# A new instruction order from a planner with a table of tile changes: top-k attention and a mixture of experts on one core

## The chip, the cores and the metric

The kernel runs on one core of a Trainium2 chip. TensorE (PE; PEld is its weight load), VectorE (DVE), ScalarE (ACT), GpSimd (POOL) and SyncE (SP, which here issues all the transfers) run side by side and meet at semaphores. The metric is the device time of one execution in microseconds (us), the median of several runs; lower is better.

## What is computed

For each of 8 batches and 8 heads (sequence 576, head width 64): scores, the 32 largest of each row kept, softmax over those, times v. The 8 heads side by side are the input x (576 x 512) of four small attention experts, each with a causal mask, and each row of x takes the two experts with the largest gate.

```python
scores = scale * np.matmul(q, k.transpose(0, 1, 3, 2))
kth = np.partition(scores, -top_k, axis=-1)[..., -top_k:-top_k + 1]
scores = np.where(scores >= kth, scores, -1000000000.0)
attn = softmax(scores)                      # top_k = 32
x = (attn @ v) as batch x 576 x 512
for e in range(E):                          # 4 experts
    q, k, v = x @ wq[e], x @ wk[e], x @ wv[e]
    a = softmax(np.where(causal, -1000000000.0, scale * (q @ k.transpose(0, 2, 1))))
    ye = a @ v @ wo[e]
    out += (gate weight of e where e is among the two chosen) * ye
```

## The kernel before

The work is cut into tasks. A task is a handful of instructions on one engine, with a duration written in the code, the tasks that it depends on, the buffers that it takes, and a priority. A planner (`Plan.order`) walks through time once when the program is built: at each step it looks, engine by engine, at the tasks that could start within `SLACK` ns of the earliest one, takes the one with the smallest priority number, and sets its end by the written duration. The order that comes out is the order of the instructions on each engine's queue. On the chip each engine works its queue strictly in that order and waits at semaphores; the planner's times are not kept. Priorities are a due time (pair of heads, plus offsets named `D_...`) plus a number for each kind of task (`BIAS`).

Two heads are one pair; 4 pairs make one batch; 32 pairs in all. Each pair has nine blocks of 128 rows (`j` = 0 to 8). The tasks that the prediction names:

- `scores` (TensorE, four matmuls into a PSUM slot, twice that for j = 4), `copy` (ScalarE, slot to SBUF `s3`), three blocks to a group.
- `f1`, `f3`, `f4`, `f5`, `win`, `rep` (VectorE): the top 32 of each row of one group of three blocks; `mask` (ScalarE).
- `s1` to `s9`: the softmax's sum. `s8` transposes it on TensorE and `s9` (ScalarE, line 726) writes it into rows of the operands that `st` reads.
- `st`: the transposed scores once more, with mask products; `exp` (ScalarE) into `pt`; `av`: times v, with 64-column weights; `neg` and `xh`, `xl`: the result as a high and a low part, x.
- Per batch, from the four pairs' x: `vproj` (5 tasks), `proj` (16), `neg2`, `s_stage` (the experts' scores), `m_stage` (VectorE, row maximum), `e_stage` (ScalarE, exponential), `t_stage` (transposes), `avm`, `c4`, `prod` (times wo), then the store.

In `s_stage` of a block t below 4, two experts are computed at once: six products with 64-row weights (`prods`), and two 128-row matmuls that add the causal mask (`causal`). In the kernel before, the planner's note `first` decides which comes first: `causal` if the task before on TensorE ended with what the planner calls short, `prods` otherwise. PSUM holds three slots and one accumulator; `s3` exists twice.

The planner knew one surcharge on TensorE:

```python
if short and t.kind not in (SHORT, TURN):
    dur += self.SWITCH          # 107 ns
t.first = short
short = t.kind in (SHORT, MIXED) or t.kind == EITHER and not short
```

Of the kernel before, what the change touches and what calls it, by code (L numbers as in the profile page):

```python
# [98 lines left out]
LONG, SHORT, EITHER, MIXED, TURN = 1, 2, 3, 4, 5  # L99


class Plan:
# [8 lines left out]
    SLACK = 35.5049  # L111
# [3 lines left out]
    SWITCH = 107.0  # L115
# [28 lines left out]
    def order(self):  # L144
        engs = {t.eng: [0.0, []] for t in self.tasks}
        port = {"DVE": -1e9, "POOL": -1e9}
        short = False
# [39 lines left out]
        while len(out) < len(self.tasks):  # L187
# [6 lines left out]
            s, _, _, t = best  # L194
# [39 lines left out]
def dve(n):  # L234
    return (n + 66) / 0.96


def pool(n):
# [5 lines left out]
BIAS = {"<lambda>": 23.740355, "again": 11.475029, "av": 0.361842, "avm": 11.263865, "c1": 7.177941, "c2": -23.286692,  # L244
        "c3": -10.384414, "c4": 6.710642, "c5": -28.708972, "cast": 24.64198, "cast_swap": -0.010375, "check1":
        -18.850708, "check2": 53.583539, "check3": -34.443475, "compare": 26.790953, "constants": 21.071669,
        "copy": -2.358499, "count": 28.676911, "diag": 14.816047, "dup": -1.633581, "dup1": -3.600648, "dup2":
# [4 lines left out]
        "load_swap": 2.335659, "loadv": -1.414793, "low_again": -18.468765, "m_stage": -40.332939, "mark":  # L252
        -1.554494, "mask": -0.719054, "neg": 2.485033, "neg2": -9.889744, "o_stage": -12.76194, "oh":
        -25.677682, "ol": 20.823251, "ot": -30.766377, "prod": 22.021447, "proj": 0.40995, "rep": -9.52529,
        "s1": -31.464437, "s2": -12.850911, "s3": -9.816986, "s4": -13.763698, "s6": -2.693483, "s7": -4.517811,
        "s8": -3.65251, "s9": -21.892878, "s_stage": 0.129474, "scores": -0.234018, "st": -0.066757, "store":
        -15.216484, "sub": 14.129481, "t_stage": -14.84831, "tails": 8.355447, "vproj": 1.194931, "win":
        11.080557, "xh": 7.528878, "xl": 7.883384}
D_K2 = 33.110076
D_PREP = -6.722199  # L260
D_SC = 0.592125
D_TIE = 20.447724
D_MASK = 0.804776
D_STAT = -3.65447
D_TAIL = 0.303862
D_STEP = 0.099275
D_MOE = 4.227275
D_LAST = 10.459609
D_PEN = 3.906984
D_SPAN = 4.076115  # L270
# [5 lines left out]
def kernel(ctx, tc, qk, vL, wq, wk, wv, wo, out):  # L276
# [122 lines left out]
    pl = Plan()  # L399
# [139 lines left out]
    def topk(w, general):  # L539
# [4 lines left out]
        for g in range(3):  # L544
# [5 lines left out]
            for n, j in enumerate(js):  # L550
# [9 lines left out]
                a = add("PE", 531 if j != 4 else 1063, scores, need, bufs=[sl, s3] + used(w, j), prio=0, kind=LONG)  # L560
# [52 lines left out]
            marks.append(add("POOL", 200, mark, [t], bufs=[c], prio=-9))  # L613
            compare_last()
            t = add("DVE", 6 * dve(72) - 45, f5, [t], bufs=[fa, c], prio=P0)
            tl = add("POOL", 200, tails, [t], bufs=[c], prio=0)
# [683 lines left out]
```

## Time and profile before

| | before |
|---|---|
| median of 3 runs | 1190.8 us (1190.08 to 1192.21) |
| the profiled execution | 1190.3 us, of which 1188.5 us from the first to the last instruction |
| TensorE busy | 1114.5 us, 94% |
| VectorE busy | 1058.8 us, 89% |
| ScalarE busy | 985.9 us, 83% |
| mean granted TensorE clock | 0.977 of full |

Busy time is the sum of instruction times; TensorE's instructions overlap and their ends are modelled, so its waits are better read as the distance between starts of successive blocks than as idle time.

### The profile page before, as it was taken

To read this page: it belongs to the slowest core of one execution; us is meant where nothing else is said; L and a number is where in the kernel's file an instruction comes from. 1 tells how busy PE (TensorE), PEld (TensorE's weight loads), DVE (VectorE), ACT (ScalarE), POOL (GpSimd) and SP (SyncE) were. 2 spreads that over 40 slices of the span, in tenths; PEclk is the share of its full clock that TensorE was granted. 3 is DMA by queue.
4 is the path that set the end of the run, shared out by engine and by line. 5 is a ranking of instruction groups with operands and counts; after the bars stand their busy time and mean duration, and the time that the engine had idled before them with its cause. 6 is when DMAs were issued, how large, how long until landed. Compare 5 with 4: busy or idle time off the path is not lost. (4 is left out here: it accounts for less than half of the span.)

```text
span 1188.5 us, 27952 instructions
## 1 busy us (share of the span) xinstructions
PE 1114.5 (94%) x9330; PEld 911.7 (77%) x9330; DVE 1058.8 (89%) x4457; ACT 985.9 (83%) x2050; POOL 374.8 (32%) x803
## 2 busy tenths in 40 slices
PE   3688799999999999999999999999999999999997
PEld 2466587877878778887878778787788878787785
DVE  7999999999999999999999999999999999999121
ACT  5687779789898888989888888988888898888554
POOL 4322221424324232253223332252322542232112
PEclk8688899999999999999999999999999999999999
DMA  7133332223432332333422233323423334220101
GB/s 198 49 92 92 92 85 74 57 72 100 114 91 68 88 101 71 82 93 87 135 69 73 64 102 105 91 78 82 115 63 82 83 101 122 67 73 15 44 5 44
DMA packets 45576, 98.54 MB, mean 83 GB/s; under 512 B 7792, under 2 KB 7792, under 8 KB 45424
## 3 DMA queue, kind: packets, MB, share of 16 engines
q1 hardware_dynamic: 45424, 96.67, 30.4%
q8 instruction: 76, 1.25, 0.5%
q14 instruction: 76, 0.62, 0.2%
HBM read 32.06 MB, written 9.44 MB: 35 GB/s over the span
## 5 line engine op out<-in xcount | busy, mean ns | idle before, releaser
L817 ACT ACTIVATE pt<-slot 128x576 f32<-128x576 f32 x288 | 183.8, 649 | 69.8 <-PE slot L291 67.5
L291 PE MATMUL slot<-opa,opa 128*128 128x256 f32 (+3 forms) x984 | 197.1, 324 | 26.1 <-ACT s L558 11.0
L648 ACT ACTIVATE mask<-s,top 128x576 bf16<-128x576 f32 x288 | 212.2, 772 | 7.3 <-DVE top L602 6.7
L590 POOL COPY scrap<-cand 128x1 f32<-128x1 f32 x96 | 18.0, 187 | 601.6 <-DVE cand L586 575.1
L291 PE MATMUL acc<-pt,vt 128*64 128x256 f32 (+3 forms) x1152 | 198.4, 423 | 1.2 <-ACT pt L817 1.2
L558 ACT ACTIVATE s<-slot 128x576 f32<-128x576 f32 x288 | 176.4, 653 | 19.4 <-PE slot L291 18.1
L291 PE MATMUL slot<-opb,opb 128*128 128x320 f32 (+1 forms) x960 | 182.7, 311 | 4.3 <-DMA opb<-raw 1.9
L291 PEld LDWEIGHTS slot<-opa,opa 128*128 128x128 f32 (+1 forms) x984 | 145.7, 195 | 45.0 <-ACT s L558 13.9
L291 PEld LDWEIGHTS slot<-opb,opb 128*128 128x128 f32 x960 | 143.6, 193 | 11.5 <-ACT opb L726 2.4
L602 DVE MAX8 top<-cand 128x8 f32<-128x160 f32 x576 | 147.6, 311 | 0.0
L291 PEld LDWEIGHTS acc<-pt,vt 128*64 128x64 f32 (+1 forms) x1152 | 89.5, 144 | 53.5 <-issue 16.8
L577 DVE MAX8 cand<-fb 128x8 f32<-128x288 f32 x288 | 130.5, 453 | 0.0
L291 PEld LDWEIGHTS <-mask 128*128 128x128 bf16 (+1 forms) x1632 | 78.1, 101 | 59.7 <-issue 49.8
L291 PE MATMUL slot<-negi,mask 128*128 128x128 bf16 (+3 forms) x1632 | 121.3, 217 | 0.3 <-ACT pt L817 0.2
L569 DVE TENSOR_TENSOR fa<-s 128x864 f32<-128x864 f32 x96 | 107.3, 1118 | 10.5 <-ACT s L558 10.5
L572 DVE TENSOR_TENSOR fb<-s 128x864 f32<-128x864 f32 x96 | 101.4, 1056 | 0.0
L628 POOL TENSOR_TENSOR ind<-cand,top 128x486 bf16<-128x486 f32 x96 | 96.2, 1002 | 7.1 <-ACT ind L636 6.9
L602 DVE MAX8 top<-oct 128x8 f32<-128x72 f32 x576 | 93.8, 218 | 0.0
L607 DVE MATCH_REPLACE8 cand<-top,cand 128x160 f32<-128x160 f32 x288 | 86.1, 309 | 0.0
L636 ACT ACTIVATE ind<-ind,tiny 128x486 bf16<-128x486 bf16 (+1 forms) x96 | 67.5, 703 | 8.3 <-POOL ind L628 7.0
L291 PE MATMUL slot<-opa,k2a 128*128 128x256 f32 (+1 forms) x320 | 69.3, 298 | 2.8 <-ACT opa L726 2.8
L291 PE MATMUL slot<-opb,k2b 128*128 128x320 f32 x320 | 70.3, 301 | 0.5
(191 smaller groups left out, 2393.4 us busy)
## 6 DMA issues: line engine op xcount, KB each, us to landing
raw<-in_qk_dram SPq DMA_DIRECT2D x31, 576.0 KB, 3.7
opb<-raw SPq DMA_DIRECT2D x93, 144.0 KB, 3.3
opa<-raw SPq DMA_DIRECT2D x93, 144.0 KB, 2.4
vt<-in_vL_dram SPq DMA_DIRECT2D x32, 320.0 KB, 3.4
opb<-opb SPq DMA_DIRECT2D x62, 144.0 KB, 2.6
opa<-opa SPq DMA_DIRECT2D x62, 144.0 KB, 2.4
out_dram<-pr SPq DMA_DIRECT2D x32, 256.0 KB, 2.0
k2a<-opa SPq DMA_DIRECT2D x32, 144.0 KB, 2.3
```

The costliest lines, as they stand in the source:

```text
L291: nc.tensor.matmul(o, l, r, start=start, stop=stop, skip_group_check=True)
L558: nc.scalar.activation(s3.t[:, n], sl.t[:, o0:o0 + S], AF.Copy)
L569: v.tensor_tensor(out=fa.t, in0=s3.t[:, :, 0:288], in1=s3.t[:, :, 288:576], op=OP.max)
L572: v.tensor_tensor(out=fb.t, in0=s3.t[:, :, 0:288], in1=s3.t[:, :, 288:576], op=OP.min)
L577: v.max(out=c.t[:, n, 152:160], in_=fb.t[:, n])
L590: nc.gpsimd.tensor_copy(scrap[:, g:g + 1], c.t[:, 0, 143:144])
L602: v.max(out=w.top.t[0][:, j, 8 * r:8 * r + 8], in_=oc.t[:, n] if r < 2 else c.t[:, n, 0:160])
L607: v.match_replace(out=c.t[:, n, 0:72] if r == 1 else src, in_values=src, imm_value=LOW, in_to_replace=w.top.t[0][:, j, 8 * r:8 * r + 8])
L628: nc.gpsimd.tensor_tensor(out=ind.t[:, 0:486].rearrange("p (a n) -> p a n", a=3), in0=c.t, in1=m32[:, js[0]:js[0] + 3, 31:32].to_broadcast ...
L636: nc.scalar.activation(ind.t[:, 0:n], ind.t[:, 0:n], AF.Sign, bias=tiny, accum_out=signs[:, 3 * w.p + g:3 * w.p + g + 1])
L648: nc.scalar.activation(w.mask[j].t, s3.t[:, n], AF.Relu, bias=w.top.t[0][:, j, 31:32], scale=-1.0)
L817: es[j] = add("ACT", act(S), lambda sl=sl, pt=pt, o0=o0: nc.scalar.activation(pt.t, sl.t[:, o0:o0 + S], AF.Exp, scale=0.125), [a], bufs=[s ...
```

## The change

Four things are edited. The surcharge becomes a table by what stood before on TensorE (`COST`, with two new kinds: `AV` for tasks with 64-column weights, `ROW` for `s_stage` below block 4). Many written durations are new. `s_stage` has `causal` first always. `f3` and `f4` no longer wait, in the planner, for GpSimd. And all the priorities (`BIAS`, `D_...`, `SLACK`) are other numbers, so that the order of the instructions on every engine is another; the instructions themselves, their operands and shapes are the same.

```diff
-    SLACK = 35.5049
+    SLACK = 58.114
-    SWITCH = 107.0
+    COST = ((0, 0, 0, 0, 0, 0, 0, 0), (0, 0, 8, 0, 0, 0, 98, 0), (0, 78, 0, 144, 150, 0, 110, 82),
+            (0, 80, 26, 82, 80, 0, 10, 28), (0, 129, 100, 115, 130, 0, 0, 53), (0, 173, 70, 65, 100, 0, 107, 0))
+    NEXT = {LONG: 1, SHORT: 2, MIXED: 3, AV: 4, ROW: 5}
...
-                elif e == "DVE" and t.tag in self.PORT:
+                elif e == "DVE" and t.tag in self.PORT and t.tag not in ("f3", "f4"):
...
-                if short and t.kind not in (SHORT, TURN):
-                    dur += self.SWITCH
-                t.first = short
-                short = t.kind in (SHORT, MIXED) or t.kind == EITHER and not short
+                dur += self.COST[state][t.kind]
+                t.first = state > 1
+                state = self.NEXT.get(t.kind, 1 if t.first else 3)
...
-BIAS = {"<lambda>": 23.740355, "again": 11.475029, "av": 0.361842, "avm": 11.263865, "c1": 7.177941, "c2": -23.286692,
+BIAS = {"<lambda>": 383.78, "again": -295.6731, "av": 1.0033, "avm": 620.4783, "c1": 108.4144, "c2": -154.7034,
...
-            a = add("PE", 1020 if j != 4 else 790, lambda j=j, pts=pts: av(j, pts), [es[k] for k in jj] + [w.v, a],
-                    bufs=pts + [acc, w.vt], prio=1, tag="av", kind=SHORT)
+            a = add("PE", 1070 if j != 4 else 727, lambda j=j, pts=pts: av(j, pts), [es[k] for k in jj] + [w.v, a],
+                    bufs=pts + [acc, w.vt], prio=1, tag="av", kind=AV)
...
-            t = add("DVE", 6 * dve(72) - 45, f5, [t], bufs=[fa, c], prio=P0)
+            t = add("DVE", 3 * dve(144) - 22, f5, [t], bufs=[fa, c], prio=P0)
...
-                        order = (causal, prods) if pl.first else (prods, causal)
-                        order[0](True)
-                        order[1](False)
+                        causal(True)
+                        prods(False)
...
-                        kind=EITHER if t < 4 else MIXED)
+                        kind=ROW if t < 4 else MIXED)
...
-                pe = (190, 360, 600, 810, 520)[t]
+                pe = (217, 430, 658, 825, 468)[t]
```

Three places show how instructions move. The first is VectorE at the program's start, before and after as one difference. Line 469 and line 499 make the low parts of the first pair's operands, lines 380 to 395 (most of them stand unchanged in the part left out) the constants, line 569 is the first `f1`.

```order
+L469 TENSOR_TENSOR opa_0_69<-raw_68,opa_2_71 64x576
+L469 TENSOR_TENSOR opa_1_70<-raw_68,opa_2_71 64x576
 L469 TENSOR_TENSOR opb_0_78<-raw_68,opb_2_80 64x576
 L469 TENSOR_TENSOR opb_1_79<-raw_68,opb_2_80 64x576
-L469 TENSOR_TENSOR opa_0_69<-raw_68,opa_2_71 64x576
-L469 TENSOR_TENSOR opa_1_70<-raw_68,opa_2_71 64x576
-L499 TENSOR_TENSOR opa_2_71<-pr_144,opa_0_69 64x576
 L380 TENSOR_SCALAR identf<-ptm_0_149 128x128
 L380 TENSOR_SCALAR identb<-ptm_0_149 128x128
```

Line 499 of `opa` stood ahead of all the constants and now stands behind them, just ahead of line 499 of `opb`. At the same place ScalarE's queue (the casts of the next pair are line 462, the copies of the first three score blocks line 558 with `s_87`) changes as follows:

```order
 L415 ACTIVATE wv_199<-ot_154 128x1040
 L558 ACTIVATE s_87<-slot_64 128x576
+L462 ACTIVATE opa_2_74<-raw_68 128x576
 L558 ACTIVATE s_87<-slot_65 128x576
 L462 ACTIVATE opb_2_83<-raw_68 128x576
 L558 ACTIVATE s_87<-slot_66 128x576
 L558 ACTIVATE s_88<-slot_64 128x576
-L462 ACTIVATE opa_2_74<-raw_68 128x576
 L558 ACTIVATE s_88<-slot_65 128x576
```

A cast, which needs the next pair's load, has moved between the first and the second copy. On SyncE the load of v (line 514) has moved ahead of the first load of q and k (line 458).

The second place is TensorE in the middle of the program, behind an `s8` (line 722). Before, one `scores` (`opb_1`, `opb_0`) stands between it and the `st` (`opb_0`, `opb_1`) that reads what `s9` writes:

```order
L722 MATMUL slot_65<-identf,stat_2_119 4x128 x4
L291 MATMUL slot_66<-opb_1_79,opb_0_78 128x320
L291 MATMUL slot_66<-opb_1_79,opb_0_78 128x256
L291 MATMUL slot_66<-opb_1_79,opb_2_80 128x320
L291 MATMUL slot_66<-opb_1_79,opb_2_80 128x256
L291 MATMUL slot_65<-opb_0_81,opb_1_82 128x320
L291 MATMUL slot_65<-opb_0_81,opb_1_82 128x256
```

In the change, at the same point of the batch's rhythm, a `neg2` (`negr`) and a `proj` (`wk`) stand between them:

```order
L722 MATMUL slot_65<-identf,stat_2_119 4x128 x4
L291 MATMUL slot_66<-qk_0_133,negr 128x288 x2
L291 MATMUL slot_64<-x_0_125,wk_197 128x288 x2
L291 MATMUL slot_64<-x_1_126,wk_197 128x288 x2
L291 MATMUL slot_64<-x_0_125,wk_198 128x288 x2
L291 MATMUL slot_65<-opb_0_81,opb_1_82 128x320
L291 MATMUL slot_65<-opb_0_81,opb_1_82 128x256
```

So the `st` has two blocks ahead of it where it had one.

The third place is TensorE at the first `s_stage` of the second two experts. Before, its products (`qk`) are followed by two `scores` and an `av` (`acc`), and, further on, by an `st`, before its transposes:

```order
L291 MATMUL slot_64<-qk_2_135,qk_0_133 128x128 x2
L291 MATMUL slot_64<-qk_2_135,qk_1_134 128x128 x2
L291 MATMUL slot_64<-qk_3_136,qk_0_133 128x128 x2
L291 MATMUL slot_65<-opb_1_82,opb_0_81 128x320
L291 MATMUL slot_65<-opb_1_82,opb_0_81 128x256
L291 MATMUL slot_65<-opb_1_82,opb_2_83 128x320
L291 MATMUL slot_65<-opb_1_82,opb_2_83 128x256
L291 MATMUL slot_66<-opb_1_82,opb_0_81 128x320
```

In the change the next `s_stage` (causal pair first: `tri`, `identb`) and one `av` stand between them and the transposes (`pr`); these rows begin inside that next `s_stage`, behind its causal pair:

```order
L291 MATMUL slot_64<-qk_2_135,qk_0_133 128x256 x2
L291 MATMUL slot_64<-qk_2_135,qk_1_134 128x256 x2
L291 MATMUL slot_64<-qk_3_136,qk_0_133 128x256 x2
L291 MATMUL acc_67<-pt_121,vt_86 64x256
L291 MATMUL acc_67<-pt_122,vt_86 64x256
L291 MATMUL acc_67<-pt_122,vt_86 64x320
L291 MATMUL acc_67<-pt_121,vt_86 64x320
L1077 MATMUL slot_66<-identf,pr_144 128x128 x2
```

Four blocks between the first scores and their transposes have become two.

## Rows read from the trace of the kernel before

**Rows 1.** The page: busy time, share of the span and instructions of each engine.

```profile
PE 1114.5 (94%) x9330; PEld 911.7 (77%) x9330; DVE 1058.8 (89%) x4457; ACT 985.9 (83%) x2050; POOL 374.8 (32%) x803
```

**Rows 2.** Windows: stretch, length, busy us of each engine (instructions), granted clock, DMA.

```profile
8.50:162.40 153.90, 113.49 (x762) 86.94 (x763) 146.39 (x643) 113.30 (x213) 44.81 (x82) 0.83 0.34 90
162.40:290.90 128.50, 123.03 (x1060) 101.03 (x1059) 122.26 (x523) 111.20 (x237) 46.33 (x96) 1.00 0.32 84
580.20:718.10 137.90, 136.43 (x1168) 112.34 (x1167) 131.48 (x554) 121.91 (x256) 45.94 (x98) 1.00 0.33 88
1086.00:1188.50 102.50, 91.09 (x788) 74.59 (x786) 27.34 (x83) 57.88 (x130) 19.00 (x45) 0.98 0.10 31
```

**Rows 3.** Timeline of VectorE at the start: start us, us, instructions [idle before <-releaser].

```profile
8.54 0.23 DVE L380 TENSOR_SCALAR identf<-ptm 128x128 f32<-128x128 int32 x1
...
10.36 0.17 DVE L395 MEMSET sm<- 128x128 f32 x1
...
14.59 1.06 DVE L569 TENSOR_TENSOR fa<-s 128x864 f32<-128x864 f32 x1 [3.27 <-ACT s L558]
...
24.14 1.55 DVE L569 TENSOR_TENSOR fa<-s 128x864 f32<-128x864 f32 x1
```

**Rows 4.** Timeline of ScalarE at the start.

```profile
10.84 1.19 ACT L558 ACTIVATE s<-slot 128x576 f32<-128x576 f32 x2
13.33 0.68 ACT L462 ACTIVATE opb<-raw 128x576 fp32r<-128x576 f32 x1 [1.30 <-DMA raw<-in_qk_dram]
```

**Rows 5.** Timeline of SyncE's DMA issues at the start.

```profile
1.66 0.43 SPq L514 DMA_DIRECT2D vt<-in_vL_dram  x1
```

**Rows 6.** Timeline of TensorE in a middle batch: blocks that follow each other without a wait.

```profile
701.79 1.64 PE L291 MATMUL slot<-wo,qk 128*128 128x512 f32 x6
703.27 1.76 PE L291 MATMUL slot<-opb,opb 128*128 128x320 f32 x12
704.96 1.19 PE L291 MATMUL acc<-pt,vt 128*64 128x256 f32 x8
706.08 0.43 PE L291 MATMUL slot<-negi,mask 128*128 128x64 bf16 x5
...
716.69 2.92 PE L291 MATMUL slot<-wo,qk 128*128 128x512 f32 x12
719.45 0.38 PE L722 MATMUL slot<-identf,stat 128*4 128x128 f32 x2
```

**Rows 7.** Timeline of TensorE in the same batch: four places with a wait.

```profile
621.90 0.53 PE L291 MATMUL acc<-x,negr 128*128 128x256 f32 x2
623.02 1.33 PE L291 MATMUL slot<-opa,opa 128*128 128x256 f32 x8 [0.59 <-DVE v L903]
...
625.96 0.77 PE L291 MATMUL slot<-opb,opb 128*128 128x320 f32 x4
626.88 0.53 PE L291 MATMUL slot<-opb,opb 128*128 128x320 f32 x2 [0.15 <-ACT opb L726]
...
692.58 0.43 PE L291 MATMUL slot<-negi,mask 128*128 128x64 bf16 x5
693.25 0.53 PE L291 MATMUL slot<-opa,opa 128*128 128x256 f32 x2 [0.24 <-ACT pt L817]
...
698.76 1.48 PE L291 MATMUL acc<-pt,vt 128*64 128x256 f32 x8
700.17 0.43 PE L291 MATMUL slot<-negi,mask 128*128 128x64 bf16 x5
```

**Rows 8.** Timeline of all engines at two `s_stage` (`tri`) and an `av` (`acc`).

```profile
604.39 0.27 PE L291 MATMUL slot<-tri,identb 128*128 128x128 bf16 x2
...
605.19 0.42 DVE L1058 TENSOR_REDUCE sm<-slot 128x2 f32<-128x256 f32 x1 [0.43 <-PE slot L291]
...
605.70 1.19 PE L291 MATMUL acc<-pt,vt 128*64 128x256 f32 x8
...
606.83 0.20 ACT L1067 ACTIVATION_READ_ACCUMULATOR pr<-slot,sm 128x1 f32 x1
```

More of the change, by code (lines that the diff above doesn't have):

```diff
@@ L242 @@
 PEF = 1.0
-BIAS = {"<lambda>": 23.740355, "again": 11.475029, "av": 0.361842, "avm": 11.263865, "c1": 7.177941, "c2": -23.286692,
-        "c3": -10.384414, "c4": 6.710642, "c5": -28.708972, "cast": 24.64198, "cast_swap": -0.010375, "check1":
-        -18.850708, "check2": 53.583539, "check3": -34.443475, "compare": 26.790953, "constants": 21.071669,
-        "copy": -2.358499, "count": 28.676911, "diag": 14.816047, "dup": -1.633581, "dup1": -3.600648, "dup2":
[4 rows of a table removed]
[L252 to L270, printed above, removed]
+BIAS = {"<lambda>": 383.78, "again": -295.6731, "av": 1.0033, "avm": 620.4783, "c1": 108.4144, "c2": -154.7034,
+        "c3": 64.2277, "c4": -414.2653, "c5": 75.0207, "cast": 374.6002, "cast_swap": 813.697, "check1": -137.7188,
+        "check2": 169.9271, "check3": 340.7893, "compare": -163.741, "constants": -66.1999, "copy": 26.3246,
+        "count": 98.315, "diag": 265.3045, "dup": 94.8531, "dup1": -364.0748, "dup2": -451.9729, "e_stage": -66.8741,
[3 rows of a table added]
+        "g8": -623.0459, "g9": -194.0866, "load_": -134.7895, "load_swap": 123.308, "loadv": -319.0325,
+        "low_again": 144.4132, "m_stage": -426.4806, "mark": 504.7814, "mask": 51.3137, "neg": -637.0257,
[3 rows of a table added]
+        "st": -0.0455, "store": 502.323, "sub": -280.9441, "t_stage": -203.2947, "tails": -31.1234,
+        "vproj": -213.9761, "win": 38.661, "xh": 185.7676, "xl": 179.4791}
@@ L271 @@
+D_K2 = -9.24057
+D_PREP = -11.27653
+D_SC = 0.55092
+D_TIE = 371.38654
+D_MASK = 2.84383
+D_STAT = -42.02577
+D_TAIL = 0.31469
+D_STEP = 0.09921
+D_MOE = 4.98429
+D_LAST = 10.17993
+D_PEN = 4.21246
+D_SPAN = 4.11854
 MP = (14,3)
@@ L559, in topk @@
                 need = w.scores[0] + w.scores[1] if j == 4 else w.scores[0 if j < 4 else 1]
-                a = add("PE", 531 if j != 4 else 1063, scores, need, bufs=[sl, s3] + used(w, j), prio=0, kind=LONG)
+                a = add("PE", 525 if j != 4 else 1061, scores, need, bufs=[sl, s3] + used(w, j), prio=0, kind=LONG)
                 cps.append(add("ACT", act(S), copy, [a], bufs=[sl, s3], prio=0))
@@ L641, in later @@
                 pl.due += 0.3
-                counts.append(add("ACT", act(516, False, 1, 1), count, [a], bufs=[ind], prio=1))
+                counts.append(add("ACT", act(489, False, 1, 1), count, [a], bufs=[ind], prio=1))
                 pl.due = keep
@@ L831, in neg @@
                 mm(acc.t[:, 256 + c0:256 + c1], negr, xb.t[0][:, c0:c1], stop=True)
-        a = add("PE", 250, neg, [c], bufs=[acc, xb], prio=1, kind=LONG)
+        a = add("PE", 264, neg, [c], bufs=[acc, xb], prio=1, kind=LONG)
         d = add("ACT", act(S), lambda: nc.scalar.activation(xb.t[1][:, 0:S], av_(), AF.Copy), [a], bufs=[acc, xb], prio=1, tag="xl")
@@ L904, in moe @@
             when(1440)
-            a = add("PE", 1436, vproj, last + wd["v"], bufs=[sl, v2] + xbs, prio=3, kind=LONG)
+            a = add("PE", 1430, vproj, last + wd["v"], bufs=[sl, v2] + xbs, prio=3, kind=LONG)
             e1 = add("ACT", act(256), ev, [a], bufs=[sl, v2], prio=3)
@@ L997, in moe @@
                     when(800)
-                    a = add("PE", 795, proj, last + wd[name] + [a], bufs=[sl, qk] + xbs, prio=3, kind=LONG)
+                    a = add("PE", 787, proj, last + wd[name] + [a], bufs=[sl, qk] + xbs, prio=3, kind=LONG)
                 def ev1(sl=sl, k=k, qk=qk):
@@ L1009, in moe @@
                 c = add("ACT", act(S), ev1, [a], bufs=[sl, qk], prio=3)
-                a = add("PE", 260, neg, [c], bufs=[sl, qk], prio=3, tag="neg2", kind=LONG)
+                a = add("PE", 265, neg, [c], bufs=[sl, qk], prio=3, tag="neg2", kind=LONG)
                 d = add("ACT", act(S), ev2, [a], bufs=[sl, qk], prio=3)
@@ L1189, in moe @@
             when(1470)
-            a = add("PE", 1385, prod, split + wd["o"], bufs=[sl, oo, o], prio=3, kind=LONG)
+            a = add("PE", 1375, prod, split + wd["o"], bufs=[sl, oo, o], prio=3, kind=LONG)
             a = add("ACT", act(512), ev, [a], bufs=[sl, o], prio=3, tag="evo")
```

28 lines of the change are left out of this document (14 added, 14 removed), and 10 rows, old and new, of the table BIAS.

## The prediction

> **What bounds the kernel now.** I read the page first, then windows by stage, then TensorE's timeline inside one batch, then the start. The page shows two nearly full engines [rows 1]: TensorE at 94% and VectorE at 89%. An average over stages says little, so the windows come next [rows 2]. Four stages differ.
>
> - To 162 us there is no expert work yet. VectorE is busy 146.4 of 153.9 us and sets the pace; the granted clock averages 0.83, so TensorE spends about a third of this stage at the lower of its two levels, 1.2 GHz, and still waits. Making TensorE's order better buys nothing here; delaying VectorE costs its full delay.
> - From 162 to 291 us the first expert work comes in; TensorE 123.0 of 128.5 us (95.7%).
> - Then come the batches in the middle, all with the same rhythm; one of them takes 137.9 us, TensorE 136.4, VectorE 131.5, ScalarE 121.9, granted clock 1.00.
> - From 1086 us the last scores are out; VectorE has almost nothing left, TensorE works off the rest.
>
> In the middle, TensorE's busy time is too kind, since the modelled ends cover waits. I therefore price a block by the distance from its start to the next block's start where nothing waits [rows 6]: `prod` 2.76 us for two = 1.38; a `prod` behind the mask products of an `st` 1.48, so that such a change costs 0.10; three `scores` ahead of an `av` 1.69, which with the same 0.10 makes 0.53 for one; `av` 1.12. A `scores` streams 1152 columns, so other full-width blocks follow by their columns: `neg` or `neg2` with 576 takes 0.27, `proj` with 1728 takes 0.79. Against these prices the same batch shows waits [rows 7]: `neg` takes 1.12 us (0.85 too long, the next `scores` has no slot yet); a `scores` behind `s8` 0.92 us (0.53 and one change of 0.10; 0.29 too long, the `st` behind it waits for `s9`); the mask products of an `st`, 576 columns, 0.67 us (0.40 too long by the columns' price, of which the row prints 0.24 as idle: no free slot until an `exp` has read one); an `av` 1.41 us (0.29 too long). The pair `s8`, `scores`, `st` occurs twice a batch in the old order. Together 0.85 + 2 x 0.29 + 0.40 + 0.29 = 2.12 us a batch, and smaller ones beside them that I put at as much again at most. So TensorE bounds the middle, with 2 to 4 us of 137.9 lost to waits, and VectorE, 6.4 us short of full, is close behind.
>
> **The change part by part.**
>
> *The causal pair first, and the tile changes.* An `s_stage` crosses from 128-row to 64-row weights once inside itself whichever part is first; only its neighbours decide what it adds outside. 34 of 80 `s_stage` blocks turn round. I counted block pairs in both orders (they are the same 1281 blocks). Full-width work behind the 64-row products falls from 13 to 1 pairs (two changes' worth, 0.20 us: -2.4 us), full-width behind `av` from 45 to 33 (-1.2), behind transposes from 76 to 61 (-1.5), `av` behind full-width from 92 to 83 (-0.9), full-width behind mask products rises from 51 to 65 (+1.4). That is -4.6 us. Against it stand pairs that the trace prices poorly or not at all: a causal pair behind 64-row products (0 to 24 pairs), transposes behind them (1 to 16), transposes behind `av` (15 to 34). Bounds: nothing, or two changes (0.20) for the first and one (0.10) for the others: 0 to +8.2 us. Sum -4.6 to +3.6; I take the middle, **-0.5 us**.
>
> A second count looks at the weights' shapes alone (128 x 128, 128 x 64, 64 x 128, 128 x 4), transposes included in the first: a middle batch has 68 changes of shape in both orders, the whole program 540 before and 551 after; at the 0.10 us of [rows 6] for each that is +1.1 us, inside these bounds. The Trainium skill, TensorEngine Tiling (Array Packing), section Tiling Modes, says that a change of tiling mode, not of tile alone, drains the engine. The trace agrees as far as [rows 6] go, and by that rule the second count would be the right one: +1.1 us instead of -0.5.
>
> *The start.* Three moves on VectorE's path. The low part of `opa` (line 499), which the second half of the first `scores` reads, now stands behind the constants, which run from 8.54 to 10.53 us [rows 3]. The first `f1` begins at 14.59 after 3.27 us of waiting for the third copy. The ScalarE cast that waits until 13.33 us for the next pair's load [rows 4] now stands ahead of the second copy, so copies two and three come behind it and behind a second cast: 13.33 + 0.68 + 0.65 + 0.68 + 0.65 = 15.99 instead of 14.59, 1.4 us later. And the load of v is issued first, 0.43 us [rows 5], which may move the load chain too. I take **+1.7 us**; bounds 0 (the constants fill VectorE's 3.27 us of idle time and the load lands earlier) and +2.5. VectorE is full from there to 162 us, so nothing takes it back.
>
> *Experts earlier.* In the new order the first `vproj` stands 8 blocks behind the fourth pair's `neg`; in the old one 57. TensorE's idle time in 162 to 291 us, 5.5 us, can shrink to the middle's rate (1.5 of 137.9 gives 1.4): up to -4.1 us. I take half, **-2.0 us**; bounds -4.1 and 0.
>
> *Waits in the middle.* No edit removes a wait by itself; the order decides. What I can place: the two s9 waits go, because behind `s8` there now stand at least two blocks (for instance `neg2` and `proj`, 0.27 + 0.79 = 1.06 us, against the 0.92 after which the `st` could start [rows 7]): -0.58. For the slot and `exp` waits (0.85, 0.40, 0.29) the order has other neighbours and I cannot tell, so half: -0.77. What speaks for that half: the written durations come nearer to the trace. `av` is now written 1070 ns and 53 to 130 for what follows (1020 before, and 107 at most; the row has 1120), `neg` 264 (250; 270 by columns), and one group of VectorE's top 32, f1 to the last `win`, adds up to 9.57 us (was 9.82; 24.14 - 14.59 = 9.55 [rows 3]). The old order was laid out for a VectorE that would be slower and a TensorE that would be faster than they are; the new one keeps ScalarE and VectorE nearer to what TensorE needs. For the smaller waits I take -0.65. A new one arises: in the second two experts the first transposes have only an `s_stage` and an `av` between them and their scores. Two such `s_stage` blocks take 605.70 - 604.39 = 1.31 us, so these two 0.66 + 1.12 = 1.78; the chain from the maximum to the second sum took 605.19 to 607.03 = 1.84 us, and the products must end before it [rows 8]. At least 0.06 is missing, 0.3 with a handover of 0.24 as behind `exp` [rows 7]; I put in half of 0.3, +0.15. Sum -1.85 us a batch. The stretch from 162 to 1086 us is 924 / 137.9 = 6.7 batches: **-12.4 us**. Bounds: all named waits and as much again in small ones go, 4.2 x 6.7 = -28; or new waits equal the old ones, 0.
>
> *GpSimd and f3, f4.* That rule is the planner's alone and moves places only. `f1` takes 1.06 us in one row and 1.55 in another [rows 3]; a few such extensions more are covered by VectorE's 6.4 us of slack a batch, so 0; without that cover each would cost its 0.5.
>
> *The end.* TensorE-bound; the same blocks in another order, 0 (bounds -2 to +4, since ten more blocks stand behind the last `scores` than before, and only 11.4 us of the last 102.5 are idle).
>
> Sum: 1190.3 + 1.7 - 0.5 - 2.0 - 12.4 = 1177.1 us for the profiled execution. The median of the runs lies 0.5 above it, so **1177.6 us**.
>
> **The rivals.**
>
> *It only moves the waits* (chance 0.13). Counted by shapes nothing is gained in tile changes (+1.1), and three slots with ScalarE at 121.9 of 137.9 us [rows 2] make TensorE wait somewhere in any order. Then 1190.8 + 1.7 + 1.1 - 2.0 = 1191.6 us, within 0.2% of before, which is about what a measurement of this kernel can tell from no change. Against it: the s9 waits have a cause that the new order takes away.
>
> *VectorE starves* (chance 0.18). A batch has 160 TensorE blocks, 0.86 us each. The longest run of blocks without a `scores` grows from 13 to 19 of them, 11.2 to 16.4 us. Three `scores` and their last copy add 1.6 + 0.65, so 18.6 us pass between one group's arrival and the next one's; a group keeps VectorE for 9.55 us, the five row maxima in that run for about 3 (my estimate from 0.42 for the smallest [rows 8]). With two `s3` buffers a full stock covers it; a group that arrives just in time leaves up to 6 us of idle time. At half of that, and with today's 6.4 us of idle unchanged, a batch takes 3 us more: 1190.8 + 1.7 + 3 x 6.7 = 1212.6 us. It decides from the point on where VectorE idles more than 6.4 us a batch.
>
> *Nearly all waits go* (chance 0.12). TensorE then runs at its blocks' prices, bounded by VectorE's 131.5: 1190.8 + 1.7 - 0.5 - 2.0 - 28 = 1162.0 us.
>
> **How the numbers follow.** The forecast's own case, waits reduced by 0.7 to 3.3 us a batch, has 0.57: its time runs from 1168 to 1185 (1190.8 + 1.7 - 0.5 - 2.0 = 1190.0, less 22 or 5). With the last rival's 0.12 faster has 0.69; within 0.2% (1188.4 to 1193.2) has 0.13, slower 0.18. The range 1163 to 1193 leaves out the upper part of the starving case, about 0.15, and half of the last rival, about 0.05.
>
> **What would show it.** A middle batch of 136.0 us instead of 137.9; no line with TensorE idle before an `st` and released by line 726; the first `f1` near 16.3 us; the first `vproj` 49 blocks of 0.86 us, some 40 us, earlier than before; TensorE's changes of tile no cheaper in sum. The prediction is wrong if the batch stays at 137 or more, or if VectorE's busy share in a batch falls while TensorE's does too.

## The result, and the profile after

The median of the changed kernel is 1175.65 us (1174.58 to 1176.66, 4 runs), that of the kernel before 1190.68; the ratio is 0.9872, with a 95% interval from 0.9855 to 0.9889. The profiled execution took 1176.66 us, 13.6 us less than the one of before; 13.2 were forecast for it.

The first line is from the page: the busy time of each engine.

```profile
PE 1101.2 (94%) x9330; PEld 908.0 (77%) x9330; DVE 1057.8 (90%) x4457; ACT 983.5 (84%) x2050; POOL 371.7 (32%) x803
```

Against [rows 1] the work of VectorE and ScalarE is the same and the shares barely move; the span is shorter. To see where, I divide both traces at marks, the `neg` of each batch's last pair. Windows of the changed kernel between such marks (columns as in [rows 2]): the first two batches with expert work, one in the middle, and the end.

```profile
163.60:299.20 135.60, 130.98 (x1136) 107.81 (x1136) 129.31 (x551) 118.64 (x250) 47.33 (x97) 1.00 0.31 82
299.20:438.20 139.00, 137.73 (x1183) 113.85 (x1182) 134.38 (x571) 124.14 (x261) 46.59 (x100) 1.00 0.34 90
573.70:708.90 135.20, 134.50 (x1167) 111.83 (x1167) 130.78 (x554) 121.05 (x256) 44.88 (x98) 1.00 0.34 90
1109.80:1174.90 65.10, 55.61 (x469) 47.77 (x468) 11.71 (x25) 31.41 (x75) 10.81 (x29) 0.98 0.09 31
```

The marks stand at 162.4, 303.0, 440.7, ... 1123.2 us before and at 163.6, 299.2, 438.2, ... 1109.8 us after. So the start costs 1.2 us in these two traces, the seven batches in between give 960.8 - 946.2 = 14.6 us, and the end 65.3 - 65.1 = 0.2 us. The first mark alone is unsteady: of the kernels below, three with the queues of before up to it reach it at 159.3, 160.4 and 163.7 us, and three with the changed kernel's queues at 161.6, 162.2 and 163.0. The means of four traces each, 161.5 and 162.6, differ by about as much as the pair does, but a difference of 1 or 2 us at this mark between two single traces says little. The batches in the middle repeat better, within 0.4 us (137.7 to 137.9 before, 135.1 to 135.5 after, but for two that are named below). A batch in the middle went from 137.9 [rows 2] to 135.2 us. Its 2.7 us can be written down for each engine: VectorE's idle time fell from 6.4 to 4.4 us and its busy time by 0.7, TensorE's idle time by 0.8 and its busy time by 1.9, ScalarE's by 1.8 and 0.9.

On TensorE, as the distance from each block's start to the next block's start, such a batch consists of:

| us a batch | before | after |
|---|---|---|
| `neg` (4) | 2.35 | 1.06 |
| `scores` (36) | 24.55 | 23.32 |
| `st` (32, without block 4) | 27.43 | 26.69 |
| `s8`, `vproj`, `proj` (29) | 24.70 | 24.00 |
| `s_stage` of blocks below 4 (8) | 6.65 | 7.03 |
| `t_stage` (10) | 5.96 | 6.54 |
| `av` (20) | 21.56 | 21.86 |
| all others | 24.68 | 24.77 |
| sum | 137.88 | 135.27 |

Two of the places whose waits were named ahead of the result, in TensorE's timeline: first `neg` (`acc`, `negr`), then `s8` and the `st` that needs it:

```profile
603.14 0.43 PE L291 MATMUL acc<-x,negr 128*128 128x256 f32 x2
603.40 0.55 PE L291 MATMUL slot<-opa,opa 128*128 128x256 f32 x3
...
611.61 0.60 PE L722 MATMUL slot<-identf,stat 128*4 128x128 f32 x4
611.97 0.51 PE L291 MATMUL slot<-qk,negr 128*128 128x288 f32 x2
612.31 0.95 PE L291 MATMUL slot<-x,wk 128*128 128x288 f32 x6
613.11 0.42 PE L291 MATMUL slot<-opb,opb 128*128 128x320 f32 x2
```

`neg` takes 0.26 us to the next `scores` where it took 1.12 [rows 7]; all four of the batch take 0.26 to 0.27. Behind `s8`, `neg2` takes 0.34 and `proj` 0.80 us, and the `st` starts with no idle time. In the whole trace TensorE waits for line 726 twice, 0.7 us together; before, it was eight times, 3.5 us.

The start: VectorE's first `f1`, then ScalarE's casts (462) and copies (558), from the timelines of the two engines.

```profile
16.99 1.06 DVE L569 TENSOR_TENSOR fa<-s 128x864 f32<-128x864 f32 x1 [2.52 <-ACT s L558]
```

```profile
14.62 0.68 ACT L462 ACTIVATE opa<-raw 128x576 fp32r<-128x576 f32 x1 [1.44 <-DMA raw<-in_qk_dram]
15.21 0.63 ACT L558 ACTIVATE s<-slot 128x576 f32<-128x576 f32 x1
15.74 0.67 ACT L462 ACTIVATE opb<-raw 128x576 fp32r<-128x576 f32 x1
16.32 2.26 ACT L558 ACTIVATE s<-slot 128x576 f32<-128x576 f32 x4
```

As the order said, the second copy stands behind a cast that waits for the load, and the first `f1` begins at 16.99 instead of 14.59 us [rows 3].

### The profile page after: what moved, and what is told of

It is laid out like the page before. It is cut to its first block, busy times and chain, and to the rows that moved or that the text cites. A ratio compares the mean times of both kernels' runs of the same rounds, so it can differ in the third digit from the quotient of the medians.

```text
span 1174.9 us, 27936 instructions
## 1 busy us (share of the span) xinstructions
PE 1101.2 (94%) x9330; PEld 908.0 (77%) x9330; DVE 1057.8 (90%) x4457; ACT 983.5 (84%) x2050; POOL 371.7 (32%) x803
## 5 line engine op out<-in xcount | busy, mean ns | idle before, releaser
L648 ACT ACTIVATE mask<-s,top 128x576 bf16<-128x576 f32 x288 | 216.8, 776 | 12.9 <-DVE top L602 12.5
L291 PE MATMUL slot<-opa,opa 128*128 128x256 f32 (+3 forms) x984 | 193.7, 323 | 24.3 <-ACT s L558 12.1
L291 PE MATMUL acc<-pt,vt 128*64 128x256 f32 (+3 forms) x1152 | 193.7, 418 | 4.2 <-ACT pt L817 4.1
L291 PE MATMUL slot<-opb,opb 128*128 128x320 f32 (+1 forms) x960 | 178.2, 308 | 0.4
L291 PEld LDWEIGHTS acc<-pt,vt 128*64 128x64 f32 (+1 forms) x1152 | 85.3, 142 | 60.2 <-issue 24.4
L569 DVE TENSOR_TENSOR fa<-s 128x864 f32<-128x864 f32 x96 | 102.1, 1064 | 16.1 <-ACT s L558 16.1
L1066 ACT ACTIVATE pr<-slot,sm 128x128 f32<-128x128 f32 (+3 forms) x120 | 62.1, 525 | 13.4 <-DVE sm L1057 12.5
```

What stands on the lines that cost most here:

```text
L291: nc.tensor.matmul(o, l, r, start=start, stop=stop, skip_group_check=True)
L569: v.tensor_tensor(out=fa.t, in0=s3.t[:, :, 0:288], in1=s3.t[:, :, 288:576], op=OP.max)
L648: nc.scalar.activation(w.mask[j].t, s3.t[:, n], AF.Relu, bias=w.top.t[0][:, j, 31:32], scale=-1.0)
L1066: nc.scalar.activation(pr.t[:, 512 * h:512 * h + w], sl.t[:, 512 * h:512 * h + w], AF.Exp, bias=mx[:, t, h:h + 1], accum_out=su[:, t, h:h ...
```

## The experiments

In all but the last two the order of the tasks is the one of the kernel named, but for the moves that are told. Ratios are against the kernel before on the same chip; the changed kernel's is 0.9872. The medians come from several chips, on which the kernel before took 1190.2 to 1192.3 us, so small differences are read from the ratios.

**The inner order of `s_stage`.** In the kernel before, causal always first:

```diff
-                        order = (causal, prods) if pl.first else (prods, causal)
-                        order[0](True)
-                        order[1](False)
+                        causal(True)
+                        prods(False)
```

> The kernel before with one edit alone: causal pair first in every s_stage of a block below 4 (34 of 80 blocks turn round), the order of the tasks untouched. Theory (the tile changes are no cheaper in sum, the gain is in the waits): no gain; of the 34 blocks those behind 64-row or full-width work win or lose up to two changes of 0.10 us, in sum between -3 and +3 us, so 1188 to 1194. Rival (the causal pair first is where the gain comes from, about a third of the change's 15 us or more): 1185.7 or less.

Measured: 1193.57 us (7 runs), ratio 1.0027 [1.0016, 1.0038], so 0.27% slower, at the upper end of what the theory allowed; a middle batch takes 138.1 us where it took 137.9 (the profiled execution is the fastest of the seven, so it does not show the whole). In the trace before, 27 of the 64 blocks below 4 have the products first, and these turn round; the 34 of 80 on record count blocks 4 as well, which have no causal pair to turn. In the changed kernel, the products always first:

```diff
-                        causal(True)
-                        prods(False)
+                        prods(True)
+                        causal(False)
```

> The changed kernel with the products always first and the causal pair second (all 80 blocks turn round), the order of the tasks untouched. In the trace after the change an s_stage behind another's 64-row products took about 0.10 us more in the first and 0.10 us more in the second than an undisturbed pair, and this edit joins products to products instead. Theory (the inner order carries nothing of the gain): within 4 us of the changed kernel, 1171.6 to 1179.6. Rival (the inner order carries a third of the gain or more): 1180.7 or more.

Measured: 1177.97 us (6 runs, 1175.9 to 1182.37), ratio 0.9899 [0.9883, 0.9915], which overlaps a little with the changed kernel's; a middle batch takes 135.4 us. The blocks that turn round are 64, not 80. The runs are spread with the clock: 1182.4 and 1182.1 us at a mean granted clock of 0.970 and 0.971, 1176.5 and 1175.9 at 0.980. Two `s_stage` and the `av` behind them, in the kernel before (from the place of [rows 8]), in the changed kernel and in this one:

```profile
604.60 0.95 PE L291 MATMUL slot<-qk,qk 64*128 64x128 f32 x12
605.48 0.28 PE L291 MATMUL slot<-tri,identb 128*128 128x128 bf16 x2
```

```profile
620.01 0.28 PE L291 MATMUL slot<-tri,identb 128*128 128x128 bf16 x2
620.22 0.55 PE L291 MATMUL slot<-qk,qk 64*128 64x128 f32 x6
620.70 0.28 PE L291 MATMUL slot<-tri,identb 128*128 128x128 bf16 x2
620.91 0.62 PE L291 MATMUL slot<-qk,qk 64*128 64x256 f32 x6
621.46 1.19 PE L291 MATMUL acc<-pt,vt 128*64 128x256 f32 x8
```

```profile
623.30 0.55 PE L291 MATMUL slot<-qk,qk 64*128 64x128 f32 x6
623.79 0.29 PE L291 MATMUL slot<-tri,identb 128*128 128x128 bf16 x2
624.00 0.62 PE L291 MATMUL slot<-qk,qk 64*128 64x256 f32 x6
624.55 0.28 PE L291 MATMUL slot<-tri,identb 128*128 128x128 bf16 x2
624.77 1.19 PE L291 MATMUL acc<-pt,vt 128*64 128x256 f32 x8
```

621.46 - 620.01 = 1.45 us and 624.77 - 623.30 = 1.47 us; before, the same two took 1.31 [rows 8], with the products of both side by side between the two causal pairs. A causal pair behind 64-row products is not free, it costs about 0.14 us, and in either inner order of all blocks alike it is paid. So the inner order is worth some 0.2 us a batch, with either sign; it carries little of the gain, as the theory said.

**The s9 wait, with another block in its place.** In the kernel before, twelve times `st` and the block behind it change places on TensorE alone:

```diff
+    q = [t for t in out if t.eng == "PE"]
+    for i in range(len(q) - 3):
+        if [t.tag for t in q[i:i + 3]] == ["s8", "scores", "st"] and q[i + 3].tag in ("s_stage", "prod"):
+            q[i + 2], q[i + 3] = q[i + 3], q[i + 2]
```

> The kernel before with twelve swaps on TensorE: wherever the queue had s8, one scores, st and then a prod or an s_stage of block 4, the st goes behind that last block, so that it no longer waits for s9. Nothing else moves. Theory (these waits are real time, 0.29 us each): no wait on line 726, and 12 x 0.29 = 3.5 us less, about 1187.3. Rival (the st arrives later at its exp and the wait turns up there or at the next slot): within 1 us of the kernel before, 1189.7 to 1191.7.

Measured: 1203.76 us, ratio 1.0126 [1.0109, 1.0142], 13.6 us slower, outside what theory or rival allowed. A middle batch takes 140.2 us. ScalarE's and TensorE's timeline at one of the six swaps with an `s_stage` (line numbers are 49 higher here: 775 is `s9`, 1135 the copy of the transposes, 866 `exp`):

```profile
629.79 0.59 ACT L775 ACTIVATE opb<-slot 4x512 fp32r<-4x512 f32 x1
...
630.39 1.02 ACT L1135 ACTIVATE ptm<-slot 128x1024 f32<-128x1024 f32 x1
...
631.47 1.05 PE L340 MATMUL slot<-qk,bd 128*128 128x288 f32 x6 [1.19 <-ACT ptm L1135]
...
632.40 0.51 PE L340 MATMUL slot<-opb,opb 128*128 128x320 f32 x2
...
633.48 0.65 ACT L866 ACTIVATE pt<-slot 128x576 f32<-128x576 f32 x1 [1.52 <-PE slot L340]
...
634.18 0.77 PE L340 MATMUL acc<-pt,vt 128*64 128x256 f32 x4 [0.16 <-ACT pt L866]
```

The block that was to cover the wait needs a slot that ScalarE frees one task later than `s9`. So it waits 1.19 us instead, the `st` behind it begins 2.0 us after its own data were there (630.38 to 632.40), ScalarE idles 1.52 us for it, and `av` comes late too. The six swaps with a `prod` did not even take the wait for `s9` away, since the `prod` needs the slot that `s9` reads:

```profile
701.78 1.65 PE L340 MATMUL slot<-wo,qk 128*128 128x512 f32 x6 [0.50 <-ACT opb L775]
```

In the whole trace TensorE waits for `s9` ten times, 5.7 us, where it was eight times and 3.5 us. So this kernel does not show what such a wait is worth; it shows that another block put ahead of it waits longer, because the slots come from the same ScalarE queue.

**The start put back in the changed kernel.**

```diff
+    move("SP", "loadv", 0, "load_", 1)
+    move("DVE", "constants", 0, "low_again", 0)
+    move("ACT", "cast", 2, "copy", 1)
+    move("ACT", "cast", 3, "copy", 3)
```

> The changed kernel with four instructions at the start put back where they stood before: the load of v behind the first two loads, VectorE's low part of opa (line 499) ahead of the constants, and two of ScalarE's casts behind the copies that they now delay. Nothing else moves. Theory (VectorE sets the pace up to the first batch, so a late first f1 is lost for good): the first f1 begins 2.4 us earlier (14.6 instead of 17.0) and the kernel ends 1.2 to 2.4 us earlier, 1173.3 to 1174.5. Rival (the delay is taken back in the first batch, where the marks already show only 1.2 us of the 2.4): within 0.8 us of the changed kernel, 1174.9 to 1176.5.

Measured: 1175.63 us, ratio 0.9881 [0.9866, 0.9895]: nothing gained. The last pair's `neg` of the first batch does come at 159.8 instead of 163.6 us (2.8 us ahead of the mean of the four traces told above), but the next batch's at 299.2 as in the changed kernel. Two things stand in between. Windows (the granted clock is the third figure from the end):

```profile
175.00:180.00 5.00, 3.40 (x26) 2.71 (x25) 5.00 (x15) 2.09 (x5) 4.40 (x4) 1.00 0.64 148
180.00:185.00 5.00, 4.85 (x28) 3.72 (x29) 5.00 (x33) 2.37 (x5) 2.34 (x8) 0.66 0.01 2
...
205.00:210.00 5.00, 4.70 (x21) 3.09 (x21) 5.00 (x30) 4.64 (x15) 2.81 (x5) 0.50 0.41 102
```

TensorE, busy 3.40 of 5 us, falls to 1.2 GHz from 180.8 to 184.3 us, and again from 204.7 to 211.6. The four timed runs have mean clocks of 0.971 to 0.973, those of the changed kernel 0.976 to 0.980. And the timeline shows why TensorE had so little to do (lines 56 higher: 992 is the exponential of the gate, 873 `exp`):

```profile
176.69 1.04 DVE L625 TENSOR_TENSOR fa<-s 128x864 f32<-128x864 f32 x1
176.71 2.60 POOL L987 TENSOR_TENSOR g<-v,g 128x20 f32<-128x20 f32 x1 [0.45 <-DVE g L982]
177.65 1.05 DVE L628 TENSOR_TENSOR fb<-s 128x864 f32<-128x864 f32 x1
...
178.62 0.60 DVE L635 TENSOR_TENSOR cand<-fa 128x432 f32<-128x432 f32 x1
...
179.34 0.22 ACT L992 ACTIVATE g<-g 128x20 f32<-128x20 f32 x1 [2.43 <-POOL g L987]
179.46 0.63 ACT L873 ACTIVATE pt<-slot 128x576 f32<-128x576 f32 x1
...
180.15 1.54 PE L347 MATMUL acc<-pt,vt 128*64 128x256 f32 x6 [1.75 <-ACT pt L873]
```

A 0.22 us instruction stands at the head of ScalarE's queue and waits 2.43 us for GpSimd, while `exp`, whose slot is full, stands behind it and `av` waits for `exp`. The changed kernel has the same place (2.43 us at 183.09 us), and in its one trace no fall of the clock behind it.

**That wait taken away.** ScalarE's small exponential goes behind the `exp` and the two masks that followed it; first with the start put back, then in the changed kernel alone.

```diff
+    i = [k for k, t in enumerate(a) if t.tag == "g5"][0]
+    a.insert(i + 3, a.pop(i))
```

> The third kernel of this study (start put back) with one more move on ScalarE: the small exponential of the first batch's gate (line 936 of the changed kernel, 128x20) goes behind the exp and the two masks that stood behind it. In that kernel's trace it waited 2.43 us for GpSimd, the av behind it on TensorE idled 1.75 us, and the granted clock stood at half from 180.8 to 184.3 and from 204.7 to 211.6 us, which in the changed kernel's trace it did not. Theory (the 3.8 us that the earlier start won at the fourth neg were given back by that idle time and the lower clock behind it): no idle av there, no half clock behind 150 us, and 3.3 + 1.75 us less than the changed kernel: about 1170.6. First rival (the dip at 205 us lowers the clock anyway): the wait goes, the half clock at 205 us stays, 1173 to 1174.5. Second rival (the first batch is bounded by something else): no change, 1175.6 within 0.8.

> The changed kernel with only that move on ScalarE: the small exponential of the first batch's gate behind the exp and the two masks. Theory (the wait is on the path): 1.75 us less than the changed kernel, about 1173.9. Rival (the block behind it waits for VectorE's next maxima anyway): within 0.8 us of it, 1174.9 to 1176.5.

Measured: 1172.46 us, ratio 0.9831 [0.9817, 0.9844], and 1173.55 us, ratio 0.9845 [0.9831, 0.9858]. The first of the two is faster than both kernels; it fell 1.9 us short of what its theory gave, and the second came out as its theory said. The first one's timeline at the place (lines 65 higher) and two windows behind it:

```profile
177.41 0.63 ACT L882 ACTIVATE pt<-slot 128x576 f32<-128x576 f32 x1
177.94 1.43 ACT L713 ACTIVATE mask<-s,top 128x576 bf16<-128x576 f32 x2
178.35 1.19 PE L356 MATMUL acc<-pt,vt 128*64 128x256 f32 x8
...
179.93 0.22 ACT L1001 ACTIVATE g<-g 128x20 f32<-128x20 f32 x1 [0.56 <-POOL g L996]
```

```profile
180.00:185.00 5.00, 5.00 (x40) 4.13 (x39) 5.00 (x31) 3.40 (x7) 2.31 (x7) 1.00 0.01 2
...
200.00:205.00 5.00, 3.50 (x32) 2.38 (x30) 5.00 (x23) 4.50 (x11) 2.59 (x4) 1.00 0.38 128
205.00:215.00 10.00, 10.00 (x84) 7.54 (x85) 8.38 (x28) 9.26 (x23) 0.22 (x2) 1.00 0.29 67
```

No `av` idles, the clock stays at 2.4 GHz, and the first batch takes 134.2 us where it took 139.4 with the start put back alone. Taking away the one wait of 1.75 us is worth 3.2 us in the medians and 0.5% in the ratios with the start put back (1175.63 to 1172.46, 0.9881 to 0.9831), and 2.1 us or 0.27% without (1175.65 to 1173.55; these intervals overlap a little). But the clock does not hang on that `av` alone: in the second kernel's trace, where no `av` idles either, it falls from 206.4 to 209.8 us.

```profile
205.00:210.00 5.00, 4.54 (x20) 2.67 (x21) 4.35 (x31) 3.29 (x11) 1.40 (x2) 0.66 0.64 148
```

What the start is worth once the wait is gone, 1.1 us, lies inside the intervals of the two.

**What paces a middle batch.** Three kernels made from the changed one, and one from the kernel before. `proj` without its last product (low part of the weights), so that part of the result is left out (each `proj` has four matmuls instead of six):

```diff
-((WT[name][0], xh), (WT[name][0], xl), (WT[name][1], xh))
+((WT[name][0], xh), (WT[name][0], xl))
```

> The changed kernel with less work for TensorE: proj leaves out the last of its three products (high part of x times low part of the weights), so that its 16 tasks a batch have 16 matmuls instead of 24; 16 x 0.26 = 4.2 us a batch. Theory (TensorE bounds the middle batches, VectorE's 131.5 us is the next bound): a middle batch goes from 135.2 to 131.0 to 132.5 us, the kernel to 1145 to 1156. Rival (the batch is paced by the chain of slots through ScalarE, and TensorE's freed time turns into waits): less than half of it comes through, a batch above 133.1, the kernel above 1160.

> The kernel before with the shorter proj (its last product left out, 4.2 us of TensorE's work a batch). In the changed kernel the same edit took 1.1 us off a middle batch. Theory (the old order loses 2.65 us a batch to TensorE, through its place in the chain of waits, and the relief gives them back): a batch falls from 137.8 by 2.5 us or more, below 135.3, and the kernel to 1172 or less. Rival (the old order loses them between ScalarE and VectorE, where TensorE's relief changes nothing): it falls by 1.1 us or less as in the changed kernel, batch 136.7 or more, kernel 1181 or more.

More work for ScalarE, and for VectorE:

```diff
+                nc.scalar.activation(ind.t[:, 0:n], ind.t[:, 0:n], AF.Sign, bias=tiny)
...
+                v.tensor_tensor(out=fb.t[:, :, 0:32], in0=s3.t[:, :, 0:32], in1=s3.t[:, :, 288:320], op=OP.min)
```

> The changed kernel with more work for ScalarE: line 636's sign (128x486, 0.70 us without its accumulator) is done twice, which changes no value. That is 12 x 0.70 = 8.4 us a batch more, and ScalarE goes from about 121.5 to 130 of 135.2 us. Theory (TensorE's waits come from ScalarE's queue, so a later copy or exp is a longer wait): a middle batch grows by a third or more of it, 2.8 us and up, and the kernel by 18 us and up, 1194 or more. Rival (ScalarE's 14 us of idle time a batch cover it): the batch stays within 0.5 us of 135.2, the kernel ends under 1180.

> The changed kernel with more work for VectorE: behind line 572 the smaller of two 96-element pieces is taken once more (no value changes). From 0.36 us for 216 elements and 0.59 for 432, 0.23 us each, 12 a batch: 2.8 us, VectorE from 130.8 to 133.6 of 135.2 us. The kernel whose proj was shortened by 4.2 us a batch came down by 1.1 us a batch alone, with VectorE as busy as before and its idle time unchanged. Theory (VectorE with the 4 us that it must wait for copies and sums paces the batch): all of it comes through, a middle batch of 137.5 to 138.2, the kernel 1175.7 + 32 x 0.7 = 1198, 1194 and up. Rival (VectorE's 4.4 us of idle time cover it): the batch stays within 0.7 us, the first four pairs alone cost 2.8 us, the kernel under 1182.

A middle batch of each as a window: the changed kernel with the shorter `proj`, the kernel before with it, ScalarE's load, VectorE's load.

```profile
570.80:704.90 134.10, 131.10 (x1136) 107.68 (x1136) 130.60 (x554) 120.73 (x256) 44.13 (x98) 1.00 0.34 91
```

```profile
575.90:712.30 136.40, 133.57 (x1135) 108.22 (x1134) 132.23 (x554) 121.40 (x256) 44.06 (x97) 1.00 0.33 89
```

```profile
582.30:720.50 138.20, 135.38 (x1168) 112.05 (x1167) 130.83 (x554) 127.98 (x268) 44.78 (x98) 1.00 0.33 88
```

```profile
582.70:719.30 136.60, 135.10 (x1168) 111.82 (x1168) 133.22 (x567) 121.56 (x256) 45.26 (x98) 1.00 0.34 89
```

| kernel | work added a batch | batch | median, ratio |
|---|---|---|---|
| changed, shorter `proj` | TensorE -4.2 (estimate) | 135.2 to 134.1 | 1166.29, 0.9773 [0.9755, 0.9791] |
| before, shorter `proj` | TensorE -4.2 (estimate) | 137.9 to 136.4 | 1176.17, 0.9873 [0.9859, 0.9887] |
| changed, second sign | ScalarE +8.5 (12 x 0.705) | 135.2 to 138.2 | 1197.15, 1.0042 [1.0025, 1.0058] |
| changed, second minimum | VectorE +3.1 (12 x 0.258) | 135.2 to 136.6 | 1189.45, 0.9985 [0.9975, 0.9995] |

A quarter of TensorE's relief comes through, 0.35 of ScalarE's load and 0.45 of VectorE's. The busy time of the windows changes by less than these sums of instruction times, by -3.4, +6.9 and +2.4 us; measured by it, the shares are 0.32, 0.43 and 0.57. By either measure no engine paces the batch by itself, and TensorE, the busiest, has the smallest share. On the shorter `proj` the rival was right, on ScalarE the theory; on VectorE neither, as half comes through. The old order's batch falls by 1.5 us where the rival allowed 1.1 and the theory asked for 2.5, nearer to the rival (the median, 1176.17 us, lies about halfway): with TensorE relieved, the two orders are still 136.4 - 134.1 = 2.3 us a batch apart, of 2.7, and the whole kernels 1.0%, of 1.3. So, for the most part, the change's gain does not hang on how much TensorE has to do.

**The planner's numbers apart.** The changed code with the old priorities and `SLACK`, and the old code with the new ones (`BIAS`, `D_...` and `SLACK` changed places, nothing else).

> The changed kernel's code (table, durations, causal pair first, the rule for f3 and f4) with the old priorities and the old SLACK. Theory (an order is made by both together; the old priorities were chosen for the old durations): little or none of the gain, 1184 to 1200. Rival (the table and the truer durations carry the gain): 1182 or less.

> The old code (one surcharge of 107 ns, old durations, inner order by the planner's note) with the new priorities and the new SLACK. Theory (an order is made by both together): little or none of the gain, 1184 to 1200. Rival (the priorities carry the gain by themselves): 1179 or less.

Measured: 1234.89 us, ratio 1.0364 [1.0348, 1.0381], and 1218.8 us, ratio 1.0241 [1.0226, 1.0256]. Both are far slower than either kernel, and slower than the theory gave. In the first a batch takes 139 to 149 us:

```profile
734.80:881.40 146.60, 139.25 (x1167) 114.71 (x1166) 130.76 (x554) 121.24 (x256) 45.31 (x98) 0.98 0.32 84
```

Its VectorE and ScalarE do the same work in 146.6 us, with 16 us of idle time on VectorE, the longest behind ScalarE's copies. The numbers are an order for one set of durations, not a quality of their own.

## Why the prediction was right, and where it was not

The sum held: -13.2 forecast, -13.6 measured on the profiled executions, 1177.6 against 1175.65 us on the medians. The path that it named, shorter waits on TensorE in the middle batches, is where the table finds the time. By its parts:

- **The start**, +1.7: the first `f1` came 2.40 us later (bound 2.5), for the reason given, and 1.2 us of it were left at the first mark. "VectorE is full from there to 162 us, so nothing takes it back" failed behind the mark: the kernel with the start put back was ahead there by 2.8 to 3.8 us and won nothing at the end. That the half clock and the idle `av` took it back is read from the traces; that they go together is not shown, since the traces have either one without the other.
- **Causal first and the tile changes**, -0.5: borne out in size; 0.2 us a batch with either sign. The price of the causal pair behind 64-row products, put between 0 and 0.20, is 0.14 [rows 8]. One reading behind the counts does not hold: the `prod` of [rows 6] that costs 0.10 more stands behind mask products, and their weights are 128 x 128 too, in bf16 instead of f32. So that 0.10 is no change of shape. The price of such a change comes out of other blocks of both traces: a `scores` takes 0.53 us ahead of another and 0.63 ahead of an `av`. A count by shapes alone leaves out the changes of type; with them I count 964 changes before and 977 after, so nothing is gained in sum by this count either. For the rule on changes of mode in the Trainium skill, TensorEngine Tiling (Array Packing), section Tiling Modes, these 0.14 us for one more crossing of row modes agree in sign. Of [rows 6], which the prediction took to agree with it, only the three `scores` ahead of an `av` bear on it.
- **Experts earlier**, -2.0, **and the waits in the middle**, -12.4: with the tile changes -14.9, and the seven batches gave -14.6. The first expert batch alone gave -5.0 and the second +1.3 (139.0 us where it was 137.7), so this term was spread otherwise than told. A middle batch gave -2.65, not -1.85; the `neg` wait went wholly (-1.29 in the table, not half of 0.85), `t_stage` grew by 0.58 where +0.15 stood, and `s_stage` by 0.38.
- **f3, f4 and GpSimd**, 0: this term was put at nothing, and `f1` became cheaper, 102.1 us instead of 107.3 over 96. Before, six `f1` from 385 us on, one a batch in the middle, run beside a GpSimd instruction on 128x576 (line 471) and take 1.92 to 2.07 us; after, the slowest behind the start takes under 1.2. So a collision that was in every middle batch has gone with the new order. It is 0.87 us of VectorE's work a batch; by the share of VectorE's load that comes through above, 0.45, I estimate that it gives 0.4 of the 2.7 us. At one of them in the kernel before:

```profile
697.85 1.43 POOL L471 TENSOR_TENSOR raw<-raw,opa 128x576 f32<-128x576 f32 x1 [0.64 <-ACT opa L462]
...
698.27 1.92 DVE L569 TENSOR_TENSOR fa<-s 128x864 f32<-128x864 f32 x1
```

- **The end**: 65.3 and 65.1 us from the last `neg`. Counted from the last `scores` it grew from 102.5 to 109.1 us, beyond the bound of +4, but only because the last `scores` come 20.2 us earlier; the mark was badly chosen.
- **"The first `vproj` 49 blocks of 0.86 us, some 40 us, earlier than before"** was wrong: it came at 165.9 instead of 169.7 us. The old order spread its five `vproj`, and I had counted to the last of them.

The step that failed is "So TensorE bounds the middle". 4.2 us less of TensorE's work shortened a batch by 1.1 us (1.5 in the old order), while loads on ScalarE and VectorE came through to a third or more, so no engine sets the pace alone. That the three slots couple them fits the trace of the swapped blocks, but was not tried by itself. The price of the s9 waits, "the two s9 waits go ...: -0.58", is neither shown nor refuted: in the new order the waits went, but the kernel that was made to take them away alone moved them and made them longer. Nor do the 2.7 us written down engine by engine name a cause, since the sum of idle and busy time must come out the same on each. Of the rivals, "only moves the waits" is out by the time, "VectorE starves" since VectorE's idle time fell, and "nearly all waits go" since the time lies some 14 us above its 1162.0. That the total came out so close is partly luck: a middle batch gave 0.8 us more than its term, the first expert batch 5.0 where -2.0 stood for that stage, the second lost 1.3, and the start's +1.7 was not found at the end when it was put back.

Open: which of the moved instructions gave the rest of the 2.7 us, since every order here is one piece; what the table, the new durations and the rule for `f3` and `f4` do apart, which no run here separates; and a batch of 136.7 us near the end of the changed kernel (844 to 981 us), where a cast waits 2.4 us for its load.

## What to carry to other kernels

Where a few buffers couple the engines, price a change of order by adding or leaving out work on each engine and watching how much comes through. Before a block is moved ahead of a wait, look whose queue frees the buffer that the block needs: here it was the queue that the wait was for, and the block waited 0.50 to 1.19 us. Look at the heads of the queues for tiny instructions that wait for a slow engine: moving one of 0.22 us was worth 0.5% in one kernel here and 0.3%, not quite clear of noise, in another. Read a mark near the start from several traces before explaining a microsecond of it. And tuned priorities belong to the durations they were tuned with: either half alone cost 2.4 to 3.6%.

## What the hardware showed that I had not expected

- GpSimd's `g` instruction on 128x20 took 2.60 us beside VectorE's `f1`, `f3` and the maximum behind them (176.69 to 179.22 us), and ended 0.1 us behind them. In the changed kernel's later batches it took 0.97 us beside an `f1`, and 0.22 us at 312.97 us beside instructions with one input. Each of the three VectorE instructions has two inputs in SBUF. The Trainium skill, GPSIMD Engine Reference, section Specifications, names just this contention; the trace agrees.
- TensorE's clock fell to 1.2 GHz behind the idle `av` in the traces of two kernels (the start put back, at 180.8 us; the products first, at 184.0 us), and in the traces of the changed kernel and the shorter `proj` in it, which have an idle `av` there too, it did not. Between 204 and 218 us it fell in six of the traces that share the new order (start put back, products first, small exponential moved, shorter `proj`, both loads), for 3.4 to 6.8 us each, and not in the changed kernel's own, nor in that of the kernel with the start put back and the exponential moved. So this differs from trace to trace, and none of the waits here explains it alone. With the products first the same program took 1175.9 us at a mean clock of 0.980 and 1182.4 at 0.970.
